# Plan times of all stages taken from a search, and the last projection issued in two parts

## The chip, the cores and the metric

The kernel runs on one core of a Trainium2 chip. The metric is the device time in microseconds of one execution. The kernel before takes 248.0 us, the median of three runs from 245.78 to 248.13. "Before" and "after" are the two kernels throughout. "Span" is the length of one traced execution; the timed run of the same execution is 1.7 us longer in all of them.

## The reference

Eight batches of windowed attention (8 heads, 576 positions, head size 64, window 32 to each side), then a gated feed-forward block with a convolution of three taps. All matmuls run in bf16 in the kernel.

```python
scores = scale * np.matmul(q, k.transpose(0, 1, 3, 2))
mask = np.abs(pos[:, None] - pos[None, :]) <= 32
attn = softmax(np.where(mask, scores, -1e9))             # shortened
x = np.matmul(attn, v)                                   # then [8, 576, 512]
h = np.maximum(x @ w_in, 0.0)                            # w_in 512 x 1024
conv_out = sum(conv_w[k] * h_shifted_by(k - 1) for k in range(3))   # shortened
out = (h * sigmoid(conv_out)) @ w_out                    # w_out 1024 x 512
```

## The kernel before

The kernel does not issue its instructions in program order. It first registers every piece of work as an `Op` with the engines that may do it, what it reads and writes, and a planned time `prio`. A list scheduler then walks a small model of the engines. At each step it finds the engine that could start something first, and among the operations that this engine could start within a slack, it takes the one with the lowest planned time. The result is one fixed order of instructions for each engine.

```python
TIMES = {
    "half": {(0, 0): (5.0, 9.0), (0, 1): (9.0, 9.0), (1, 0): (26.0, 7.0), (1, 1): (33.0, 7.0)},
    "piece": [(14.0, 1.0), (25.0, 0.6), (30.0, 0.8), (37.0, 0.8)],
    "chunk": 44.0, "step": 17.7, "margin": 7.0,
    "out": (25.0, 30.0, 31.0),
    "cast": {"w_in": 11.0, "w_out": 28.0},
    "load": ["qk00", "v00", "w_in0", "w_in1", "qk01", "v01", "qk10", "w_out0", "v10", "w_out1", "qk11", "v11"],
    "ahead": (9.0, 6.0), "cast_ahead": (0.5, 4.0),
}
# ... in Plan.place():
    lim = first[0] + self.SLACK[e]
    op = min((o for o in cand if opts[o][2] == e and opts[o][0] <= lim),
             key=lambda o: (o.prio, o.idx))
# ... in attention(b), for each half s:
    scores(b, s, 0, when(b, s, 0.32))
    scores(b, s, 1, when(b, s, 0.40))
# ...
    for g in range(NP):
        values(b, s, g, when(b, s, 0.58 + 0.1 * g))
```

The attention of a batch is done in two halves: casts on ACT or POOL, transposes of q and k on PE, scores (PE), exponentials (ACT), masks (DVE or POOL), values (PE), normalised copies `xn` (DVE), and a second transpose to `xT` (on PE for batches 0 and 1, as a DMA transpose from batch 2 on). Two batches make three chunks of 384 rows for the feed-forward part: hidden matmuls (PE), relu (ACT), convolution as matmuls with diagonal weights (PE), a third tap on DVE from chunk 2 on, tanh (ACT), a product (DVE), and the projection (PE, ACT copy, store). Chunks 0 and 1 are cut into two pieces each, numbered 0 to 3, so that work can begin early. `half` and `piece` place these stages, `out` places the three projections of chunk 0, `chunk` and `step` everything from chunk 2 on.

```python
def project(c, i, t):
    # ...
    def mm(e):
        for m in range(MB):                       # MB = 8
            nc.tensor.matmul(ps(sl, 0, d_model), gT[ig][:, m, 128 * i:128 * i + 128],
                             w_out_sb[:, m, :], start=(m == 0), stop=(m == MB - 1))
    add(pe(d_model, MB), t, mm,
        reads=[("gT", ig, m, (i, x)) for m in range(MB) for x in (False, True)]
        + [("w_out", m) for m in range(MB)], ...)
```

A projection is one operation of eight matmuls, so its first matmul waits for all eight blocks of `gT`. Where PE would idle in the first 36 us of the plan, `warm` puts "spin" matmuls whose result nobody reads.

The softmax here doesn't subtract the row's maximum and nothing guards it: scores larger than these inputs give would overflow.

## Time and profile before

All of the work on PE, priced at what single matmuls take in the trace, is 200.9 us. The table gives three marks in PE's stream. "Lost" is the time of the mark less the priced work that PE has done by then. The prediction shows how the prices come out of the profile.

| mark in the kernel before | time, us | work done, us | lost, us |
|---|---|---|---|
| first hidden matmul | 18.92 | 2.7 | 16.2 |
| piece 1 | 34.36 | 13.7 | 20.7 |
| chunk 2 | 73.70 | 43.9 | 29.8 |
| end of PE | 241.7 | 200.9 | 40.8 |
| end of span | 245.2 | | 44.3 |

Two thirds of the loss falls before chunk 2. What follows is 148 us of steady work with two engines near 70 to 77% and PE nearly full.

### The profile page before, as it was taken

The numbers are of one execution on the slowest core, as the hardware profiler recorded it, in microseconds if no ns is written. First come the engines' busy times: TensorE is split into PE (matmuls) and PEld (weight loads), VectorE is DVE, ScalarE is ACT, GpSimd is POOL, SyncE is SP. The second block draws the span as 40 slices with busy tenths as digits, with TensorE's granted clock in tenths as the row PEclk, the third lists the DMA queues.
The fourth block names the chain that finished last, engine by engine and source line by source line (L and its number), as shares of the span: only waits on it lengthen the run. The fifth ranks groups of instructions, "written<-read, shape, count | busy, mean of one in ns | idle before, by whom it ended". The sixth has DMA issues, their size and how long they took to land.

```text
span 245.2 us, 6624 instructions
## 1 busy us (share of the span) xinstructions
PE 223.2 (91%) x2532; PEld 136.3 (56%) x2562; DVE 175.3 (72%) x413; ACT 173.5 (71%) x351; POOL 155.4 (63%) x154
## 2 busy tenths in 40 slices
PE   4779789996989998999999999999899999999974
PEld 2438566775746564555465655555455555555531
DVE  7675773574888797859595958887886778667640
ACT  4678895799537888686868695878577786766641
POOL 3278789979998898999977749596836070000000
PEclk9999999999799999999999999999999999999999
DMA  5999999999987899969279975979623312321213
GB/s 179 253 401 244 271 307 266 281 311 277 253 183 194 225 237 258 254 174 261 67 247 182 233 188 178 194 220 184 168 41 100 88 43 67 78 86 43 88 43 128
DMA packets 68884, 45.93 MB, mean 187 GB/s; under 512 B 53980, under 2 KB 54004, under 8 KB 68852
## 3 DMA queue, kind: packets, MB, share of 16 engines
q1 hardware_dynamic: 68816, 45.50, 69.6%
q8 instruction: 20, 0.33, 0.6%
q14 instruction: 12, 0.10, 0.1%
q10 hardware_dynamic: 36, 0.01, 0.0%
HBM read 32.52 MB, written 9.44 MB: 171 GB/s over the span
## 4 chain that ended last, share of the span: by engine, by line
PE 76%; DVE 8%; ACT 5%; issue 3%; DMA 3%; POOL 2%; SPq 1%; ACTq 0%; POOLq 0%; DVEq 0%
PE ps_all L674 24%; PE ps_all L746 23%; PE ps_all L704 14%; PE ps_all L545 6%; PE ps_all L453 5%; PE ps_all L503 3%; DVE attn L527 3%; DMA vst<-in_v_dram 3%; ACT attn L516 2%; DVE gT L726 1%; ACT kT L263 1%; SPq L353 1%; POOL qn L265 1%; DVE xn L565 1%; PE ps_all L585 1%
## 5 line engine op out<-in xcount | busy, mean ns | idle before, releaser
L674 PE MATMUL ps_all<-xT,w_in_sb 128*128 128x385 bf16 (+4 forms) x448 | 77.1, 304 | 2.3 <-DVE xT L269 0.7
L746 PE MATMUL ps_all<-w_out_sb,gT 128*128 128x512 bf16 x262 | 65.0, 379 | 3.7 <-DVE gT L726 2.4
L726 DVE SCALAR_TENSOR_TENSOR gT<-ps_all,hT 128x384 bf16<-128x384 f32 (+3 forms) x112 | 54.1, 492 | 17.7 <-ACT ps_all L723 16.8
L527 POOL TENSOR_TENSOR attn<-attn,mask 128x1024 bf16<-128x1024 bf16 x24 | 51.3, 2158 | 20.4 <-ACT attn L516 15.8
L723 ACT ACTIVATE ps_all<-ps_all 128x384 f32<-128x384 f32 (+3 forms) x112 | 49.1, 445 | 20.1 <-DVE ps_all L719 14.2
L719 DVE SCALAR_TENSOR_TENSOR ps_all<-hT,conv_w_sb,ps_all 128x384 f32<-128x384 bf16 x80 | 48.4, 613 | 15.5 <-PE ps_all L704 14.6
L690 ACT ACTIVATE hT<-ps_all 128x385 bf16<-128x385 f32 (+4 forms) x112 | 48.9, 458 | 11.1 <-PE ps_all L674 8.6
L674 PEld LDWEIGHTS <-w_in_sb 128*128 128x128 bf16 x448 | 40.4, 98 | 22.5 <-issue 2.4
L704 PE MATMUL ps_all<-hT,diag_w 128*128 128x384 bf16 (+3 forms) x256 | 51.0, 300 | 0.3 <-ACT hT L690 0.2
L746 PEld LDWEIGHTS <-gT 128*128 128x128 bf16 x288 | 27.9, 97 | 32.7 <-issue 2.6
L265 POOL TENSOR_SCALAR vo<-vst 64x1024 bf16<-64x1024 f32 (+1 forms) x36 | 35.7, 993 | 10.4 <-DMA vst<-in_v_dram 7.7
L516 ACT ACTIVATE attn<-ps_all 128x1024 bf16<-128x1024 f32 (+1 forms) x40 | 37.1, 954 | 1.7 <-PE ps_all L503 1.2
L757 ACT COPY y<-ps_all 128x512 f32<-128x512 f32 x36 | 21.1, 588 | 22.2 <-PE ps_all L746 20.8
L565 DVE TENSOR_TENSOR xn<-ps_all,rec 128x256 bf16<-128x256 f32 (+1 forms) x64 | 29.4, 482 | 0.3
L265 POOL TENSOR_SCALAR ve<-vst 128x512 bf16<-128x512 f32 (+1 forms) x39 | 23.7, 619 | 3.9 <-DMA vst<-in_v_dram 3.4
L704 PEld LDWEIGHTS <-diag_w 128*128 128x128 bf16 x256 | 20.3, 98 | 9.1 <-issue 0.6
L263 ACT COPY kT<-ps_all 128x512 bf16<-128x512 bf16 (+1 forms) x30 | 21.9, 755 | 4.3 <-PE ps_all L453 4.3
L269 DVE COPY qT<-ps_all 128x512 bf16<-128x512 bf16 (+1 forms) x27 | 20.3, 763 | 2.7 <-PE ps_all L453 2.7
L527 DVE TENSOR_TENSOR attn<-attn,mask 128x1024 bf16<-128x1024 bf16 (+1 forms) x16 | 16.4, 1035 | 8.2 <-ACT attn L516 8.1
L545 PEld LDWEIGHTS <-attn 128*64 128x64 bf16 x640 | 14.1, 115 | 12.9 <-issue 7.1
L265 POOL TENSOR_SCALAR kn<-kst 128x1152 bf16<-128x1152 f32 (+1 forms) x18 | 17.9, 1000 | 5.2 <-DVE gT L726 2.6
L545 PE MATMUL ps_all<-ve,attn 128*64 128x65 bf16 x384 | 18.1, 202 | 2.6 <-DVE attn L527 1.1
(49 smaller groups left out, 170.5 us busy)
## 6 DMA issues: line engine op xcount, KB each, us to landing
qst<-in_q_dram SPq DMA_DIRECT2D x32, 288.0 KB, 5.3
kst<-in_k_dram SPq DMA_DIRECT2D x32, 288.0 KB, 5.1
out_dram<-y SPq DMA_DIRECT2D x36, 256.0 KB, 2.2
vst<-in_v_dram SPq DMA_DIRECT2D x23, 256.0 KB, 5.6
vst<-in_v_dram SPq DMA_DIRECT2D x16, 192.0 KB, 5.8
wst<-in_moe_w_in_dram SPq DMA_DIRECT2D x2, 1024.0 KB, 8.6
wst<-in_moe_w_out_dram SPq DMA_DIRECT2D x2, 1024.0 KB, 8.8
xT<-xn SPq DMA_TRANSPOSE x30, 3.1
```

What stands on the lines that cost most here:

```text
L265: nc.gpsimd.tensor_scalar(out=out_, in0=in_, scalar1=1.0, scalar2=0.0, op0=ALU.mult, op1=ALU.add)
L516: add(act(2 * w), t + 0.1, lambda e: nc.scalar.activation(at, ps(sl, 0, 1024).rearrange("p (e x) -> p e x", e=2)[:, :, 0:w], AF.Exp, bias= ...
L527: lambda e: ENG[e].tensor_tensor(out=x_, in0=x_, in1=m_, op=ALU.mult),
L545: nc.tensor.matmul(ps(sl, (D + 1) * (n * h_ + x), (D + 1) * (n * h_ + x + 1), 64 * j, 64 * j + 64), attn[a][:, 512 * h_ + col:512 * h_ + c ...
L565: add(dve(2 * n * D), t + 0.1, lambda e: nc.vector.tensor_tensor(out=xn[i][:, cs[0]:cs[0] + n].rearrange("p c (e g) d -> p c e g d", e=2)[ ...
L674: nc.tensor.matmul(ps(sl, 0, n), w_in_sb[:, kc, m * 128:(m + 1) * 128], x_[:, kc, a0:a1], start=(kc == 0), stop=(kc == KC - 1),)
L690: nc.scalar.activation(o_, i_, AF.Relu, bias=0.0, scale=0.5)
L704: nc.tensor.matmul(ps(sl, 0, no), diag_w[:, kk, m, :], hview(m, o0, o1, kk - 1), start=(kk == 0), stop=(kk == 2),)
L719: add(("DVE", no / 960.0 + 0.13), tt + 0.1, lambda e, m=m, mid=mid, pv=pv: nc.vector.scalar_tensor_tensor(out=pv(), in0=mid, scalar=conv_w ...
L723: add(act(no), tt + 0.2, lambda e, sl=sl: nc.scalar.activation(ps(sl, 0, no), ps(sl, 0, no), AF.Tanh, bias=0.0, scale=1.0), writes=[sl], s ...
L726: add(dve(no), tt + 0.3, lambda e, m=m, mid=mid, i2=i2, pv=pv: nc.vector.scalar_tensor_tensor(out=gT[ig][:, m, o0:o1].rearrange("p (i x) - ...
L746: nc.tensor.matmul(ps(sl, 0, d_model), gT[ig][:, m, 128 * i:128 * i + 128], w_out_sb[:, m, :], start=(m == 0), stop=(m == MB - 1),)
```

## The change

The intent is to let a search choose all planned times, instead of setting them by hand. It runs on the scheduler's own model with durations varied at random, so that the order found does not hang on exact durations. Constants that were fixed (phases within a half, lags within a chunk, slacks, early starts, the batches in which q and k copies are bound to an engine) become parameters. Besides, the projection of the last chunk is cut into matmuls 0 to 5 and 6 to 7, so that most of it need not wait for the last blocks of `gT`. No arithmetic changes.

```diff
-    "half": {(0, 0): (5.0, 9.0), (0, 1): (9.0, 9.0), (1, 0): (26.0, 7.0), (1, 1): (33.0, 7.0)},
-    "piece": [(14.0, 1.0), (25.0, 0.6), (30.0, 0.8), (37.0, 0.8)],
-    "chunk": 44.0, "step": 17.7, "margin": 7.0,
-    "out": (25.0, 30.0, 31.0),
-    "cast": {"w_in": 11.0, "w_out": 28.0},
-    "load": ["qk00","v00","w_in0","w_in1","qk01","v01","qk10","w_out0","v10","w_out1","qk11","v11"],
-    "ahead": (9.0, 6.0), "cast_ahead": (0.5, 4.0),
+    "half": {(0, 0): (27.75, 1.28), (0, 1): (-3.95, 3.99), (1, 0): (24.21, 2.64), (1, 1): (46.04, 3.6)},
+    "piece": [(-0.09, 1.6), (27.99, 0.33), (36.27, 0.86), (40.99, 2.81)],
+    "chunk": 56.82, "step": 15.6, "margin": 2.54,
+    "out": (15.31, 27.98, 29.58),
+    "cast": {"w_in": 11.95, "w_out": 32.67},
+    "load": ["qk00","v00","qk01","w_in1","v01","w_in0","qk10","w_out0","v10","w_out1","v11","qk11"],
+    "ahead": (5.65, 4.52), "cast_ahead": (11.32, 0.34),
+    "phase": (-0.13, 0.27, 0.32, 0.66, 0.67, -0.07, 1.2),   # was 0.05 .32 .40 .47 .58 .10 .98
+    "lag": (2.21, 2.77, 2.38),                              # was 1.4 2.7 2.6
+    "flex": (3, 2),                                         # was: bound for b > 1
+    "slack": (0.01, 0.03, 0.04, 0.49, 0.1),                 # was 0.05 0.1 0.1 0.3 0.3
+    "early": (0.0, 0.1, 0.0),                               # was 0.12 0.04 0.04
# ... in project():
-        def mm(e):
-            for m in range(MB):
+        for m0, m1 in ((0, 6), (6, MB)) if c == NCH - 1 else ((0, MB),):
+            def mm(e, m0=m0, m1=m1):
+                for m in range(m0, m1):
# ...
-        add(pe(d_model, MB), t, mm, reads=... all eight m ..., alloc=sl, group=gr)
+            add(pe(d_model, m1 - m0), t + m0, mm, reads=... m0 to m1 ...,
+                alloc=None if m0 else sl, group=gr if m1 == MB else None)
```

(Layout of the tables is drawn together; the rest of the diff passes the new parameters to the places where the constants stood.)

More of the change, by code (lines that the diff above doesn't have):

```diff
@@ L18 @@
 TIMES = {
-    "half": {(0, 0): (5.0, 9.0), (0, 1): (9.0, 9.0), (1, 0): (26.0, 7.0), (1, 1): (33.0, 7.0)},
-    "piece": [(14.0, 1.0), (25.0, 0.6), (30.0, 0.8), (37.0, 0.8)],
-    "chunk": 44.0,
-    "step": 17.7,
-    "margin": 7.0,
-    "out": (25.0, 30.0, 31.0),
-    "cast": {"w_in": 11.0, "w_out": 28.0},
-    "load": ["qk00", "v00", "w_in0", "w_in1", "qk01", "v01", "qk10", "w_out0", "v10", "w_out1", "qk11", "v11"],
-    "ahead": (9.0, 6.0),
-    "cast_ahead": (0.5, 4.0),
+    "half": {
+        (0, 0): (27.75, 1.28),
+        (0, 1): (-3.95, 3.99),
+        (1, 0): (24.21, 2.64),
+        (1, 1): (46.04, 3.6),
+    },
+    "piece": [(-0.09, 1.6), (27.99, 0.33), (36.27, 0.86), (40.99, 2.81)],
+    "chunk": 56.82,
+    "step": 15.6,
+    "margin": 2.54,
+    "out": (15.31, 27.98, 29.58),
+    "cast": {
+        "w_in": 11.95,
+        "w_out": 32.67,
+    },
+    "load": [
+        "qk00",
+        "v00",
+        "qk01",
+        "w_in1",
+        "v01",
+        "w_in0",
+        "qk10",
+        "w_out0",
+        "v10",
+        "w_out1",
+        "v11",
+        "qk11",
+    ],
+    "ahead": (5.65, 4.52),
+    "cast_ahead": (11.32, 0.34),
+    "phase": (-0.13, 0.27, 0.32, 0.66, 0.67, -0.07, 1.2),
[3 more added lines that the diff above has]
+    "early": (0.0, 0.1, 0.0),
 }
@@ L56 @@
     ENGINES = ("PE", "ACT", "DVE", "POOL", "SP", "ACTQ")
-    SLACK = {"PE": 0.05, "ACT": 0.1, "DVE": 0.1, "POOL": 0.3, "SP": 0.3, "ACTQ": 0.1}
     def __init__(self, banks=8):
@@ L90 @@
     LAT = {"PE": 0.22, "ACT": 0.16, "DVE": 0.13, "POOL": 0.2, "SP": 0.0, "ACTQ": 0.0}
-    EARLY = {"PE": 0.12, "ACT": 0.04, "DVE": 0.04, "POOL": 0.0, "SP": 0.0, "ACTQ": 0.0}
     def place(self):
@@ L105, in place @@
         free = {"PE": 1.5, "ACT": 2.8, "DVE": 3.9, "POOL": 3.3, "SP": 0.8, "ACTQ": 0.8}
+        early = dict(zip(("PE", "ACT", "DVE"), TIMES["early"]))
+        slack = dict(zip(self.ENGINES, TIMES["slack"] + (0.1,)))
         bank = [0.0] * (self.banks - 1) + [WARM[1]]
@@ L132, in place @@
                 for e, d in op.on.items():
-                    s = max(r + self.EARLY[e] if r > 0.0 else r, free[e])
+                    s = max(r + early.get(e, 0.0) if r > 0.0 else r, free[e])
                     if best is None or s + d < best[1] - 1e-9:
@@ L139, in place @@
             e = first[2]
-            lim = first[0] + self.SLACK[e]
+            lim = first[0] + slack[e]
             op = min(
@@ L443, in transposes @@
             sl = Slot(1)
-            t = when(b, s, 0.05 * n_)
+            t = when(b, s, TIMES["phase"][0] * n_)
             n = j1 - j0
@@ L466, in transposes @@
             on = dict([("ACT", 0.00095 * 128 * n + 0.1), ("DVE", 128 * n / 960.0 + 0.08)])
-            if b > 1:
+            if TIMES["flex"][0] <= b < TIMES["flex"][1]:
                 e = "ACT" if n_ % 2 else "DVE"
@@ L616, in attention @@
             transposes(b, s)
-            scores(b, s, 0, when(b, s, 0.32))
-            scores(b, s, 1, when(b, s, 0.40))
+            scores(b, s, 0, when(b, s, TIMES["phase"][1]))
+            scores(b, s, 1, when(b, s, TIMES["phase"][2]))
             if s == 1:
-                scores(b, s, None, when(b, s, 0.47))
+                scores(b, s, None, when(b, s, TIMES["phase"][3]))
             for g in range(NP):
-                values(b, s, g, when(b, s, 0.58 + 0.1 * g))
+                values(b, s, g, when(b, s, TIMES["phase"][4] + TIMES["phase"][5] * g))
             for c in ((0, 1), (2, 3, 4))[s]:
-                turn(b, c, when(b, s, 0.98 + 0.01 * c))
+                turn(b, c, when(b, s, TIMES["phase"][6] + 0.01 * c))
         if b == 0:
@@ L707, in mm @@
                     )
-            tt = t + (m + 1.4) * dt
+            tt = t + (m + TIMES["lag"][0]) * dt
             add(pe(no, len(TAPS(c))), tt, mm, reads=hk + [("diag", kk, m) for kk in TAPS(c)], writes=[sl], alloc=sl,
@@ L742, in project @@
         gr = []
-        def mm(e):
-            for m in range(MB):
-                nc.tensor.matmul(
-                    ps(sl, 0, d_model), gT[ig][:, m, 128 * i:128 * i + 128], w_out_sb[:, m, :],
-                    start=(m == 0), stop=(m == MB - 1),
-                )
-        add(pe(d_model, MB), t, mm,
-            reads=[("gT", ig, m, (i, x)) for m in range(MB) for x in (False, True)]
-            + [("w_out", m) for m in range(MB)],
-            writes=[sl], alloc=sl, slots=[sl], group=gr)
+        for m0, m1 in ((0, 6), (6, MB)) if c == NCH - 1 else ((0, MB),):
+            def mm(e, m0=m0, m1=m1):
+                for m in range(m0, m1):
+                    nc.tensor.matmul(
+                        ps(sl, 0, d_model), gT[ig][:, m, 128 * i:128 * i + 128], w_out_sb[:, m, :],
+                        start=(m == 0), stop=(m == MB - 1),
+                    )
+            add(pe(d_model, m1 - m0), t + m0, mm,
+                reads=[("gT", ig, m, (i, x)) for m in range(m0, m1) for x in (False, True)]
+                + [("w_out", m) for m in range(m0, m1)],
+                writes=[sl], alloc=None if m0 else sl, slots=[sl], group=gr if m1 == MB else None)
         r = NYY[0] % NY
@@ L798 @@
             if c == 0:
-                t = (25.0, 30.0, 31.0)[i]
+                t = TIMES["out"][i]
             else:
-                t = start[c + 1] + (2.7 + 2.6 * i) * dm
+                t = start[c + 1] + (TIMES["lag"][1] + TIMES["lag"][2] * i) * dm
             project(c, i, t)
```

## The prediction

> **What bounds the kernel now.** I read the page first (busy shares, the 40 slices, the groups), then busy time per stage in windows, then the chain of waits from 50 to 75 us, and last the timeline of the tail.
>
> ```profile
> span 245.2 us, 6624 instructions
> ...
> PE 223.2 (91%) x2532; PEld 136.3 (56%) x2562; DVE 175.3 (72%) x413; ACT 173.5 (71%) x351; POOL 155.4 (63%) x154
> ...
> PE   4779789996989998999999999999899999999974
> ```
>
> TensorE is the only engine that could be the bound as a whole, and after slice 12 it is nearly full. But 91% busy overstates it, as matmuls overlap. So I count columns. The page and the chain give unit prices: eight 512-wide output projections in 1.73 us (216 ns each), four 385-wide hidden matmuls in 0.66 us (165 ns), nine transposes in 0.50 us (56 ns), 32 score matmuls in 0.58 us (18 ns), 24 value matmuls in 0.50 us (21 ns). With these prices the whole useful stream (448 hidden, 256 convolution, 288 projection, 288 transposes, 576 scores, 640 values, 40 second transposes, without the spin matmuls that only keep the clock up) is 200.9 us. The span is 245.2, so 44.3 us are lost, and what the change can win is among these.
>
> ```profile
> 0.00:10.00 10.00, 5.09 (x24) 2.74 (x25) 7.29 (x43) 4.85 (x7) 2.46 (x9) 1.00 0.81 186
> 10.00:20.00 10.00, 7.85 (x100) 4.64 (x101) 6.08 (x13) 6.69 (x12) 7.14 (x11) 1.00 1.10 359
> 20.00:30.00 10.00, 8.47 (x138) 6.91 (x137) 7.37 (x15) 8.77 (x20) 8.47 (x13) 1.00 1.03 271
> 30.00:40.00 10.00, 8.92 (x161) 7.39 (x160) 7.33 (x20) 9.02 (x28) 8.13 (x12) 1.00 1.04 297
> 40.00:50.00 10.00, 9.78 (x118) 6.79 (x118) 4.48 (x14) 6.18 (x14) 9.51 (x13) 1.00 0.97 272
> 50.00:60.00 10.00, 8.15 (x155) 6.45 (x153) 5.26 (x10) 10.00 (x21) 8.60 (x8) 1.00 1.04 286
> ```
>
> Columns: PE, weight loads, DVE, ACT, POOL, clock, DMA share, GB/s. ACT is near full from 20 to 40 and wholly full from 50 to 60, with a hole of 3.8 us at 40 to 50. The hole is the plan's doing: there the 24 projections of chunk 0 run as one block (39.06 to 44.4), which feed ACT nothing but three copies. DMA is saturated to 60 us.
>
> Placing the useful work (by the order of matmuls in the program) against the trace: the first hidden matmul starts at 18.9 us with 2.7 us of work done, so 16.2 lost; piece 1 of chunk 0 at 34.4 with 13.7 done, 20.7 lost; piece 3 at about 51 with 29.3, 21.8 lost; chunk 2 at 73.7 with 43.9, 29.8 lost; the last chunk at 221.8 with 182.7, 39.1 lost. TensorE ends at 241.7 (40.8 lost), and 3.5 us of last copy and store follow. So 30 of 44 us go before chunk 2, 8 of them between 51 and 74. There the chain reads:
>
> ```profile
> 56.09 1.25 ACT kT L263 x2
> 57.34 0.90 ACT attn L516
> ...
> 58.26 0.97 DVE attn L527 x2
> ...
> 67.99 2.31 DVE attn L527
> ...
> 70.63 0.50 PE ps_all L585 x8
> ```
>
> Exponentials and masks of batch 1's second half come late; its last mask ends at 70.3, then come the transposes of xn, and only then can chunk 2 begin. From chunk 2 on the loss is 9.3 us in 148, thinly spread. In the tail TensorE waits for the last gT and then does all three projections:
>
> ```profile
> 234.04 0.82 PE L704 MATMUL ps_all<-hT,diag_w 128*128 128x384 bf16 x4
> 236.34 5.34 PE L746 MATMUL ps_all<-w_out_sb,gT 128*128 128x512 bf16 x23 [1.48 <-DVE gT L726]
> ```
>
> **The Trainium skill.** "TensorE: Matmul & The Clock Gate" (section "Wait — 56ns, not 53.3ns?") gives N over 2.4 GHz plus about 2.5 ns for a warm matmul, 215.7 ns at 512; the trace's 216 ns agrees, which is why columns may be priced. The same page ("The HAM clock gate") says an idle window of some 3.4 us drops the clock to half. The trace agrees loosely: the clock reads 0.71, 0.50 and 0.94 in the three 2-us windows from 60 us, after four microseconds in which PE was busy 60%, not idle; about 1.6 us are lost. "PSUM — Partial Sum Buffer" ("Engine vs sequencer instructions") says that ScalarE, VectorE and GpSimd queues are strict FIFO and matmuls complete in program order. So a badly placed instruction holds up everything behind it on its engine; the 24 projections ahead of other work at 39 us show it. "Perfetto Trace Analysis" ("Identifying the Most-Contended Engine") warns against matmul busy share as a measure; here 91% busy stands against 82% priced work.
>
> **The change, part by part.** No arithmetic goes. The instruction orders show the same 2,536 useful matmuls, 112 tanh, 112 relu, 40 masks; spin matmuls fall from 24 to 18. Spins only fill waiting time, so I count nothing for them.
>
> First, the head. Loads: the second half of batch 0's q and k now comes before w_in, and w_in's second half before its first. The transposes and scores of that half (1.7 us) are put before the first hidden matmul. Tracing it by the trace's durations: ACT casts two vo tiles (0.62 each) before the first exponential, so that starts near 12.6 instead of 11.98; two exponentials and two masks of 0.97 end near 15.5; the values of g=3,2 come first and need the second mask; then 9 transposes of k, copies (0.75), 40 scores, and the xn copies with a 1 us mask in between. First hidden near 21.3 instead of 18.9. Work done before it is 4.4, so 16.9 lost: 0.7 worse.
>
> Second, from there to piece 1: 8.7 us of TensorE work; ACT has 8 relu and 8 tanh of 0.36, 4 casts of w_in of 0.61, 3 copies of 0.73 and one of 0.58, some 11 us. ACT is the limit: piece 1 at 30 to 31, with 13.1 done, 17.4 lost against 20.7. The loss shrinks by 3.3 in total, though two exponentials (2 us of ACT) are now still to come.
>
> Third, piece 1 to chunk 2: 28 us of TensorE work and, summed from ACT's new order, 29.5 us of ACT (24 relu and 21 tanh of 0.2 to 0.3, 9 exponentials, 7 copies, 3 xT, 4 y). Before, the like took 39.3 us. The projection block now stands after all scores of batch 1, where ACT has its exponentials to do; piece 2's work follows piece 1 with no projections between. POOL's 35 us of casts and masks to the same point and the loads (about 11.3 MB up to w_out, which the trace had moved by about 41 us) allow it. At some 85% efficiency it takes 34 us: chunk 2 at about 65 instead of 73.7, with 41.0 done instead of 43.9. Lost 24.0 against 29.8: 5.8 us won, all head parts included.
>
> Fourth, the steady part: the same mix per chunk (9.3 us lost in 148). The order frees the choice of engine for q and k copies; ACT gets 9 copies more and DVE 8 fewer, some 6.5 us of work moved, neither engine at its limit there (both 70 to 77% busy). I give it 0.5 us.
>
> Fifth, the tail. The built order is 6, 6, 2, 6, 2, 2: twelve matmuls that need only m up to 5, 2.6 us, cover the 1.9 us that the last two convolutions need through DVE, ACT and DVE. So the wait of 1.48 us goes. Against it the last copies of 0.59 come 0.43 us apart and two stores overlap, some 0.4 us. Net 1.1.
>
> Sum: 5.8 + 0.5 + 1.1 = 7.4 us; span 245.2 to 237.8. The timed median is 2.8 us above the traced span, so 240.6 us.
>
> **The rivals.** (a) The head stays bound by its loads and by ACT: DMA share is 1.0 up to 60 us and ACT 10.00 of 10. Then the order cannot pull chunk 2 ahead by more than what the hole of 3.8 us gives; with the later first hidden the gain is 2 to 3 us, and the time 245. For it: exactly these two rows. Against: the hole itself, and the late chain at 51 to 74, which is order and not load. (b) In-order stalls: the plan was found on a model, and where real durations differ (a mask took 2.31 us at 67.99 against a mean of 1.04) every engine waits behind one misplaced item, such as 40 scores before the first hidden, or the projection block waiting for w_out. This would add 3 to 6 us in the head, and the time is 246 to 249. Jittered durations in the search speak against it. (c) The steady loss falls as well, from 9.3 to 5, and the clock drop at 60 us goes: 234 to 236. For it: a search over all stages should see the whole; against: the steady part has little idle left (0.2 to 0.7 us in 20).
>
> **Range and chances.** (a) and (b) have about one chance in four together, (c) one in six. So 240.6, range 235 to 246; faster by over 2% (below 243.0) 0.74, within 2% 0.24, slower 0.02.
>
> **What would show it.** Right: first hidden later (21 to 22 us), chunk 2's first 385-wide hidden at 62 to 67 us, no row of 10 us between 30 and 60 in which ACT falls to 6, no wait of PE for the last gT over 0.3 us, last copies 0.5 to 0.6 us apart. Wrong: chunk 2 at 70 or later, PE waiting over 2 us for w_out casts or kT copies in the head, or a loss beyond 11 us between chunk 2 and the end. The largest assumption is the 85% in the third step.

## The result, and the profile after

The kernel after takes 237.45 us (median of four runs, 237.19 to 238.5) against 248.06 for before in the same rounds. The ratio is 0.960, with a 95% interval of 0.953 to 0.966, and the result is correct. Ratios are the mean time of one kernel's fast runs over that of the other's of the same rounds, so they are not quite the ratio of the medians quoted. The traced spans are 245.2 and 235.7 us: 9.5 us less.

The head of the page after, and then the row of granted clock of the page before, which the prediction left out:

```profile
span 235.7 us, 6684 instructions
...
PE 222.7 (94%) x2556; PEld 134.6 (57%) x2556; DVE 169.1 (72%) x405; ACT 179.3 (76%) x360; POOL 154.8 (66%) x153
...
PE   3897999899989999999999999999999999999993
...
PEclk9999999999999999999999999999999999999999
```

```profile
PEclk9999999999799999999999999999999999999999
```

PE's busy time is the same (222.7 against 223.2) in a span 9.5 us shorter: idle time went, not work. The row of slices has its gaps filled in the first third. And the clock of before has a dent in slice 11 that after does not have; whether the plan has a part in that one stays open, and I come back to it.

The stages of the head in the kernel after (the columns are PE, weight loads, DVE, ACT, POOL, clock, DMA share, GB/s, as in the prediction's rows of before):

```profile
10.00:20.00 10.00, 8.75 (x142) 5.28 (x141) 5.84 (x14) 8.71 (x13) 6.24 (x10) 1.00 1.14 299
20.00:30.00 10.00, 9.37 (x126) 7.35 (x126) 7.70 (x19) 8.77 (x22) 8.46 (x14) 1.00 1.08 315
30.00:40.00 10.00, 9.94 (x174) 8.83 (x172) 6.83 (x22) 9.99 (x35) 6.97 (x10) 1.00 0.96 269
40.00:50.00 10.00, 9.17 (x129) 6.88 (x128) 7.77 (x18) 8.68 (x21) 9.75 (x13) 1.00 1.11 309
50.00:60.00 10.00, 9.82 (x157) 7.03 (x156) 6.13 (x16) 7.26 (x14) 9.67 (x10) 1.00 0.89 273
```

ACT's hole of 40 to 50 us is gone (8.68 instead of 6.18), and so is the stretch of 50 to 60 in which it was full; its work is spread, and PE is at 9.2 to 9.9 of ten from 20 us on. Chunk 2 can be told by its 385-wide hidden matmuls. The timeline of PE, before and then after:

```profile
73.70 0.83 PE L674 MATMUL ps_all<-xT,w_in_sb 128*128 128x385 bf16 x4
```

```profile
21.24 1.47 PE L699 MATMUL ps_all<-xT,w_in_sb 128*128 128x256 bf16 x12 [0.48 <-DVE xT L294]
...
30.86 1.97 PE L699 MATMUL ps_all<-xT,w_in_sb 128*128 128x129 bf16 x28
...
47.35 5.34 PE L771 MATMUL ps_all<-w_out_sb,gT 128*128 128x512 bf16 x24
...
62.60 1.48 PE L699 MATMUL ps_all<-xT,w_in_sb 128*128 128x385 bf16 x8
```

| mark | before: time, lost | after: time, work done, lost | predicted for after |
|---|---|---|---|
| first hidden | 18.92, 16.2 | 21.24, 4.4, 16.8 | 21.3, lost 16.9 |
| piece 1 | 34.36, 20.7 | 30.86, 13.1, 17.75 | 30 to 31, lost 17.4 |
| chunk 2 | 73.70, 29.8 | 62.60, 41.05, 21.55 | about 65, lost 24.0 |
| end of PE | 241.7, 40.8 | 232.02, 200.9, 31.1 | |

The first line says why the time of a mark alone misleads: the first hidden matmul comes 2.3 us later, but nearly as much work has been done before it. The third line of the timeline shows that the block of 24 projections is not gone: it has moved from 39.06 to 47.35 us.

What bounds the head now can be read from the chain of waits up to chunk 2 in the kernel after:

```profile
41.13 7.54 DMA vst<-in_v_dram
...
49.24 1.31 POOL kn L290
50.55 1.17 POOL ve L290 x2
...
54.76 1.16 POOL qn L290
...
55.97 0.40 PE ps_all L478 x4
```

The chain comes from a load of v (and before that from the load and the casts of w_out), through POOL's casts, to the transposes of q, and from there stays with PE. In the kernel before the chain at this place ran through exponentials and masks.

The tail after, PE and then ACT in one view each, followed by the first of before's last three copies, which stood 1.73 us apart:

```profile
226.02 0.82 PE L729 MATMUL ps_all<-hT,diag_w 128*128 128x384 bf16 x4
226.68 5.34 PE L771 MATMUL ps_all<-w_out_sb,gT 128*128 128x512 bf16 x24
```

```profile
229.90 0.59 ACT L782 COPY y<-ps_all 128x512 f32<-128x512 f32 x1 [1.69 <-PE ps_all L771]
231.63 1.07 ACT L782 COPY y<-ps_all 128x512 f32<-128x512 f32 x2 [1.14 <-PE ps_all L771]
```

```profile
238.26 0.59 ACT L757 COPY y<-ps_all 128x512 f32<-128x512 f32 x1 [2.04 <-PE ps_all L746]
```

The 24 projections start before the last convolutions are off the pipeline, with no wait. In before there were 1.48 us of it. The last two copies stand close together (1.07 us for two), so the end after PE is 3.7 us instead of 3.5. From the start of the last convolutions to the end of the span it is 11.16 us before and 9.68 after, a gain of 1.5 us net.

So the 9.5 us are: 8.2 before chunk 2, 1.5 in the tail, and -0.2 in the 150 us between. These are two single traces. Other traces of the same two orders lost 28.0 and 28.2 us by chunk 2 (e1 and e7, order of before) and 22.2 (e5, order of after; 24.7 in e2's slow execution of it), so the 8.2 is known to some 2 us only. Up to about 1.6 of it may belong to the dent of the clock; the experiments bear on that.

### The profile page after: what moved, and what is told of

Same layout as the page of the kernel before. It is cut to its first block, busy times and chain, and to the rows that moved or that the text cites. A ratio compares the mean times of both kernels' runs of the same rounds, so it can differ in the third digit from the quotient of the medians.

```text
span 235.7 us, 6684 instructions
## 1 busy us (share of the span) xinstructions
PE 222.7 (94%) x2556; PEld 134.6 (57%) x2556; DVE 169.1 (72%) x405; ACT 179.3 (76%) x360; POOL 154.8 (66%) x153
## 4 chain that ended last, share of the span: by engine, by line
PE 65%; DMA 13%; SPq 6%; POOL 5%; DVE 3%; issue 3%; ACT 2%; ACTq 0%; POOLq 0%
PE ps_all L771 21%; PE ps_all L699 21%; PE ps_all L729 11%; DMA vst<-in_v_dram 7%; PE ps_all L570 5%; PE ps_all L478 4%; DMA wst<-in_moe_w_out_dram 4%; PE ps_all L528 3%; SPq L378 3%; DMA kst<-in_k_dram 2%; SPq L409 2%; SPq L601 1%; POOL vo L290 1%; POOL ve L290 1%; POOL w_out_sb L290 1%
## 5 line engine op out<-in xcount | busy, mean ns | idle before, releaser
L699 PE MATMUL ps_all<-xT,w_in_sb 128*128 128x385 bf16 (+4 forms) x448 | 78.6, 304 | 1.2 <-ACT xT L288 0.7
L771 PE MATMUL ps_all<-w_out_sb,gT 128*128 128x512 bf16 x288 | 67.4, 379 | 0.0
L715 ACT ACTIVATE hT<-ps_all 128x385 bf16<-128x385 f32 (+4 forms) x112 | 49.7, 459 | 10.1 <-PE ps_all L699 9.5
L771 PEld LDWEIGHTS <-gT 128*128 128x128 bf16 x288 | 27.3, 98 | 29.5
L290 POOL TENSOR_SCALAR vo<-vst 64x1024 bf16<-64x1024 f32 (+1 forms) x34 | 33.0, 971 | 4.0 <-DMA vst<-in_v_dram 1.4
L290 POOL TENSOR_SCALAR kn<-kst 128x1152 bf16<-128x1152 f32 (+1 forms) x19 | 19.2, 1012 | 11.9 <-DMA kst<-in_k_dram 8.5
L729 PEld LDWEIGHTS <-diag_w 128*128 128x128 bf16 x256 | 21.2, 97 | 9.8 <-issue 0.3
L552 DVE TENSOR_TENSOR attn<-attn,mask 128x1024 bf16<-128x1024 bf16 (+1 forms) x16 | 15.0, 944 | 8.9 <-ACT attn L541 8.8
L570 PEld LDWEIGHTS <-attn 128*64 128x64 bf16 x640 | 13.3, 111 | 11.6 <-issue 9.2
L290 POOL TENSOR_SCALAR qn<-qst 128x1152 bf16<-128x1152 f32 (+1 forms) x18 | 18.7, 1045 | 0.7 <-PE ps_all L699 0.2
L570 PE MATMUL ps_all<-ve,attn 128*64 128x65 bf16 x384 | 17.4, 197 | 0.8 <-ACT hT L715 0.7
L288 ACT COPY qT<-ps_all 128x640 bf16<-128x640 bf16 (+1 forms) x24 | 17.4, 754 | 0.3
```

The lines of the kernel that those rows point to most:

```text
L290: nc.gpsimd.tensor_scalar(out=out_, in0=in_, scalar1=1.0, scalar2=0.0, op0=ALU.mult, op1=ALU.add)
L552: lambda e: ENG[e].tensor_tensor(out=x_, in0=x_, in1=m_, op=ALU.mult),
L570: nc.tensor.matmul(ps(sl, (D + 1) * (n * h_ + x), (D + 1) * (n * h_ + x + 1), 64 * j, 64 * j + 64), attn[a][:, 512 * h_ + col:512 * h_ + c ...
L699: nc.tensor.matmul(ps(sl, 0, n), w_in_sb[:, kc, m * 128:(m + 1) * 128], x_[:, kc, a0:a1], start=(kc == 0), stop=(kc == KC - 1),)
L715: nc.scalar.activation(o_, i_, AF.Relu, bias=0.0, scale=0.5)
L729: nc.tensor.matmul(ps(sl, 0, no), diag_w[:, kk, m, :], hview(m, o0, o1, kk - 1), start=(kk == 0), stop=(kk == 2),)
```

## The experiments

All were correct, and all ran three to five rounds beside the kernel before. Variants are written in the changed source with old values put back. With all old values and no split, the order built is that of the kernel before on every engine. Each expectation names its own theories. The three groups of parameters used below are: **loads** (`load`, `cast`, `ahead`, `cast_ahead`), **head** (`half`, `piece`, `out`), **steady** (`chunk`, `step`, `margin`, `lag`, `phase`).

| run | median (range, runs), us | ratio to before, 95% interval | span, us | chunk 2: time, lost |
|---|---|---|---|---|
| e1 split alone | 245.39 (243.68 to 248.45, 6) | 0.9995 [0.990, 1.009] | 242.0 | 71.94, 28.0 |
| e2 after, no split | 239.64 (237.97 to 241.65, 6) | 0.9745 [0.968, 0.981] | 239.9 | 65.76, 24.7 |
| e3 loads on before | 243.68 (241.96 to 243.92, 4) | 0.991 [0.984, 0.998] | 242.1 | 70.51, 26.3 |
| e4 late block on before | 242.59 (240.35 to 243.51, 4) | 0.987 [0.979, 0.995] | 240.9 | 64.18, 25.0 |
| e5 after again | 238.34 (235.77 to 239.66, 6) | 0.963 [0.956, 0.970] | 236.2 | 63.23, 22.2 |
| e6 after, old loads | 243.51 (243.07 to 244.34, 4) | 0.988 [0.982, 0.994] | 241.9 | 73.70, 27.3 |
| e7 before, spins doubled | 247.14 (244.80 to 248.30, 6) | 1.001 [0.995, 1.008] | 243.5 | 72.13, 28.2 |
| e8 after, no spins | 239.90 (238.94 to 240.29, 4) | 0.974 [0.967, 0.981] | 237.2 | 63.92, 22.9 |
| e9 after, old steady | 243.35 (243.03 to 244.25, 4) | 0.984 [0.978, 0.990] | 241.3 | 70.50, 27.3 |
| e10 after, old head | 242.67 (241.84 to 244.51, 4) | 0.982 [0.975, 0.989] | 240.2 | 58.24, 20.5 |
| e11 after, block spread | 237.36 (236.63 to 237.88, 6) | 0.959 [0.954, 0.964] | 235.9 | 62.57, 22.4 |
| e12 loads and steady on before | 240.46 (240.00 to 241.34, 4) | 0.972 [0.965, 0.979] | 239.0 | 60.38, 22.7 |

The kernel before had 11 runs beside each of three sets (e1 to e4, e5 to e8, e9 to e12), each set on one chip: medians 247.56, 247.44 and 248.02.

### The split by itself: e1 and e2

e1 adds only the split to the kernel before; e2 takes only the split from the kernel after.

```diff
-        for m0, m1 in ((0, MB),):                                          # before
+        for m0, m1 in ((0, 6), (6, MB)) if c == NCH - 1 else ((0, MB),):   # e1; e2 is the reverse
```

> The kernel before, with nothing changed but the last projection in two parts (the built order is the same up to the last 24 matmuls). My theory: the wait of TensorE for the last gT (1.48 us before) goes, and 0.3 to 0.5 us of it is given back because the last two copies come 0.43 us apart and two stores overlap: 0.8 to 1.3 us faster. The rival: the end is set by the last copies and stores, which then run into each other, so that less than 0.4 us is won.

> The kernel after with the last projection in one part again, plan times kept (same order up to the last 24 matmuls). My theory: 0.8 to 1.3 us slower than the kernel after (so a ratio to the kernel before of about 0.964 instead of 0.960), all of it in a wait of TensorE for the last gT. The rival: as in the other run, under 0.4 us.

The timing of e1 says nothing either way (ratio 0.9995 with an interval of nearly 2%). The trace does, for e1's order is that of before up to the last 24 matmuls. The ends of PE's timeline, e1 and then e2:

```profile
232.26 0.82 PE L706 MATMUL ps_all<-hT,diag_w 128*128 128x384 bf16 x4
232.91 5.34 PE L748 MATMUL ps_all<-w_out_sb,gT 128*128 128x512 bf16 x24
```

```profile
228.81 0.82 PE L706 MATMUL ps_all<-hT,diag_w 128*128 128x384 bf16 x4
231.12 5.34 PE L748 MATMUL ps_all<-w_out_sb,gT 128*128 128x512 bf16 x24 [1.48 <-DVE gT L728]
```

With the split the projections follow the convolutions at once, without it comes the wait of 1.48 us, in either plan. From the last convolutions to the end it is 9.74 us (e1) and 9.68 (after) with the split, 11.16 (before) and 11.09 (e2) without. The split is worth 1.4 us in the traces, a little over the 0.8 to 1.3 expected, in either plan. The timed runs agree, though they are not all of one chip: e2's four fast runs at a mean clock of 0.999 or more have a mean of 239.1 us, those of after (seven, counting e5 below, at 0.998 or more) 237.5. The trace of e2 must not be compared as a whole. It is of an execution with a dent in the clock at 22 to 28 us, and lost 24.7 by chunk 2 instead of 21.55 with the same order.

### One group on the kernel before: e3 and e4

```diff
-    "cast": {"w_in": 11.0, "w_out": 28.0},                                 # e3
-    "load": ["qk00","v00","w_in0","w_in1","qk01","v01","qk10","w_out0","v10","w_out1","qk11","v11"],
-    "ahead": (9.0, 6.0), "cast_ahead": (0.5, 4.0),
+    "cast": {"w_in": 11.95, "w_out": 32.67},
+    "load": ["qk00","v00","qk01","w_in1","v01","w_in0","qk10","w_out0","v10","w_out1","v11","qk11"],
+    "ahead": (5.65, 4.52), "cast_ahead": (11.32, 0.34),
```

> The kernel before with only four of the new plan values: the order of loads, the two cast times, and the two lead times of loads and casts. All stage times stay old. In the built order the first hidden matmul then has 4.4 us of work before it (as in the kernel after) and the 24 projections of chunk 0 move from behind 18.3 to behind 28.2 us of work, so the block moves with no stage time changed. My theory as predicted (stage times make the gain, the loads only allow it): at most 3 us faster, since the phases, steps and half times are the old ones. The rival, that the loads are what moves the head: 5 us or more faster, and chunk 2 begins at 66 us or earlier with 44.2 us of work done.

The new loads alone win 0.9%, of some 4%. They lost 26.3 us by chunk 2, 3.5 less than before did and 1.7 less than e1, which has before's order up to there. (Each of these traces has dents ahead of chunk 2: one in e3, at 17.5 to 20.9 us, one in before, two in e1.) PE then waits for POOL's casts of q (1.9 us at the longest): new loads under the old planned times do not meet the work that they are for.

```diff
-    "out": (25.0, 30.0, 31.0),
+    "out": (50.0, 50.5, 51.0),                                             # e4
```

> The kernel before with only the three plan times of chunk 0's projections raised from 25 to 31 up to 50 to 51, loads unchanged. In the built order the block begins behind 22.2 us of work instead of 18.3 and batch 1's second-half scores come earlier (behind 28.8 instead of 32.0). My theory, that the hole of 3.8 us in ACT behind an early block and the late scores cost the 8 us between 51 and 74 us: 3 to 5 us faster, ACT without a row under 8 in 40 to 50. The rival, that the loads and their casts hold the head: within 1.5 us of the kernel before.

The same row as that with before's hole of 6.18, in e4:

```profile
40.00:50.00 10.00, 10.00 (x153) 7.75 (x151) 6.63 (x20) 7.67 (x20) 9.50 (x13) 1.00 1.10 289
```

Only half of the hole is filled (7.67; I had expected at least 8), PE is full, and 1.3% is won (3.6 us by the means of fast runs, inside the 3 to 5 expected). This shows that the block of projections at 39 us did cost time in the kernel before. It does not show by which way: when it moves, the scores of batch 1 come earlier too (from 32.0 to 28.8 us of priced work ahead of them), and the two are not separated.

### The clock and the loads: e5 to e8

e5 is the kernel after again, as a control on this chip.

> The kernel after once more, unchanged, as the control on this chip: ratio 0.955 to 0.967. By the theory that the kernel before loses part of its time to clock drops, which vary from run to run (its eleven last runs range from 244.5 us at mean clock 1.000 to 249.9 at 0.978), the runs of this kernel lie within 1.5 us of each other at a clock of 0.997 or more. The rival, that the drops are chance and fall on both kernels: a spread of 4 us or more here too.

It repeats the result: 0.963, with 22.2 us lost by chunk 2. The expectation on its spread failed: its six runs range over 3.9 us, from 235.77 (clock 0.998) to 239.66 (0.992), and one of 239.35 had 0.999. So this kernel meets a drop of the clock too, if rarely, and most of its spread comes without one.

e6 is the kernel after with the old group of loads (e3's diff, reversed).

> The kernel after with the old order of loads, cast times and lead times of loads and casts; all else new. In the built order the first hidden matmul stands behind 2.7 us of work again, the 24 projections of chunk 0 behind 17.7 us, the second-half scores of batch 1 behind 33.6. If the gain of the head is mainly the order that the loads decide (block and scores), most of it goes: 242 us or more. If the loads are worth what they gave alone on the kernel before (0.9%), it is 2 to 3 us slower than the kernel after, 239.5 to 240.5.

Windows and timeline of e6:

```profile
40.00:50.00 10.00, 9.46 (x107) 6.21 (x105) 3.87 (x13) 4.96 (x13) 9.67 (x13) 1.00 1.00 290
```

```profile
73.70 0.83 PE L676 MATMUL ps_all<-xT,w_in_sb 128*128 128x385 bf16 x4
```

The hole in ACT is back (4.96), and chunk 2 starts at 73.70, to the digit where before has it, though with 2.5 us more work done by then. All of e6's timed runs had the full clock, so the clock has no part in it. Without the new loads the new plan keeps little of its gain: the mean of e6's runs is 243.6 us, against 237.5 for the fast runs of the kernel after. As e3 won only 0.9% with them, loads and plan must be set together.

e7 asks whether the dent of the clock is a matter of PE being idle, by doubling the spins of before; e8 takes all spins from after.

```diff
-            for _ in range(n):
+            for _ in range(2 * n):        # e7;   e8: range(0)
```

> The kernel before with two spin matmuls for each one (48 instead of 24, all in the first 36 us). If the clock drops of the head come from too little TensorE activity there, the mean clock rises to 0.993 or more in every run and the median falls by 1 to 2 us, to about 246. The rival: the added spins stand in front of real work in TensorE's queue, and the time stays or grows by 1 to 3 us.

> The kernel after without any spin matmul, all else in the same order. If activity holds the clock, the mean clock falls to 0.97 to 0.985 and the time rises by 2 to 5 us over the kernel after. The rival, that the denser new order holds the clock by itself, as my prediction took for granted when it counted nothing for the spins: within 1 us of the kernel after.

The dent in the trace of before, in windows of 2 us:

```profile
58.00:60.00 2.00, 1.24 (x24) 1.09 (x24) 1.74 (x2) 2.00 (x6) 1.92 (x3) 1.00 0.98 281
60.00:62.00 2.00, 1.35 (x42) 1.27 (x42) 1.86 (x9) 1.00 (x5) 1.92 (x2) 0.71 0.91 293
62.00:64.00 2.00, 2.00 (x44) 1.57 (x44) 0.90 (x3) 1.11 (x3) 1.92 (x4) 0.50 0.97 338
64.00:66.00 2.00, 1.74 (x29) 1.53 (x25) 1.96 (x9) 1.35 (x4) 1.84 (x3) 0.94 1.26 235
```

e7's timing did not move (1.001), and its six runs had mean clocks of 1.0, 1.0, 0.993, 0.984, 0.993 and 0.986: the dents did not go. The spins fill only the first 36 us of the plan, and the dent of before's trace lies at 60. But the execution of e7 that was traced happened to have none. In it chunk 2 stands at 72.13 with 28.2 lost, 1.6 less than the 29.8 of before, which is what the prediction read off the windows as the cost of the dent. A third trace warns against taking this as settled: e1 has the same order up to there and two dents (10.9 to 14.3 and 58.7 to 62.1 us), and lost only 28.0. What a dent costs depends on where it falls, and one trace of an order differs from the next by as much.

Of e8's expectations, the slowdown came true and its reason did not. The reported clock stays at 0.998 or more without spins, yet the kernel is slower than e5, by 1.0 us in the traces, by 2.4 us in the means of fast runs on the same chip (239.8 against 237.4) and so by 1.1% in the ratios. The first hidden matmuls of e8 and of e5:

```profile
21.75 2.72 PE L676 MATMUL ps_all<-xT,w_in_sb 128*128 128x256 bf16 x12 [0.78 <-DVE xT L271]
```

```profile
21.13 1.47 PE L699 MATMUL ps_all<-xT,w_in_sb 128*128 128x256 bf16 x12 [0.78 <-DVE xT L294]
```

The same twelve matmuls take 2.72 us instead of 1.47. Without spins PE runs at about half its rate until about 24 us, while the clock column of these windows reads 1.00. In e5 the nine transposes at 5.53 us take 1.14 us and the nine at 8.94 us 0.68, so there the change to full rate came by 9 us. With spins, too, the moment differs between executions: in the trace of after, the nine transposes at 9.26 us still take 1.14 us and five spins at 12.21 us take 2.31, and the nine at 14.32 us, with 0.97, stand at the change. By chunk 2 the traces of e8 and e5 are only 0.7 us apart in loss.

How much of the whole gain do the dents make? The kernel before ran 33 times in these sets, 23 fast. Among the fast runs, six had a mean clock of at least 0.998, with a mean of 244.8 us; six near 0.993 had 246.4, and eleven near 0.985 had 247.3. The mean of all 23 is 246.4. The kernel after ran ten times, eight of them fast, all of these at 0.997 or more, with a mean of 237.5. The steps have a reason that the clock records of the traces show: all ten dents ahead of PE's end in the traces of these runs are alike, 3.41 to 3.42 us at half clock (in before's trace from 60.85 to 64.26 us). One costs 1.7 of some 245 us of clock, so a mean of 0.993 is one dent, 0.985 two and 0.978 three; the six runs of before at 0.977 to 0.979, all of them slow, have a mean of 249.2 us. That is some 1.5 us for each dent on average, with much scatter: the fast runs near 0.993 range from 244.74 to 247.79, those near 0.985 from 245.25 to 248.25.

Without dents the kernels are 244.8 - 237.5 = 7.3 us apart. The other 246.4 - 244.8 = 1.6 us go with before having dents and after hardly any. This is observed and not tried: no kernel of mine took the dents away from before, so why the plan after meets fewer of them stays open. PE is busy only 1.20 and 1.24 of 2 us ahead of the dent in before's trace, which would suit an idle PE as the cause. But the traces speak against so simple a rule. In e7 PE is less busy still at this place, 2.20 of 4 us, and no dent follows:

```profile
57.00:61.00 4.00, 2.20 (x36) 1.78 (x32) 2.11 (x3) 4.00 (x9) 3.83 (x4) 1.00 0.90 226
```

In e5, the kernel after itself, PE is busy 1.66 of 4 us from 12 to 16 us, and the clock stays (the nine transposes at 16.01 us take 0.68 us). What the runs do show is that the plan matters: e6 and e8 have no dent in four runs each, by their clocks, while e9 and e10 below have one or two in every run (e11, on the chip of these two, in one run of six).

### Which times matter: e9 to e12

e9 and e10 take one group from the kernel after: e9 puts back the old `chunk`, `step`, `margin`, `lag` and `phase`, e10 the old `half`, `piece` and `out`.

```diff
-    "chunk": 56.82, "step": 15.6, "margin": 2.54, ...                      # e9
+    "chunk": 44.0, "step": 17.7, "margin": 7.0, ...
```

> The kernel after with the old chunk start, step, margin, lags and phases (the values that place the steady part and the order within each half attention). Theory one, from the priced work (9.3 us lost between chunk 2 and the end of TensorE before, 9.5 after, 1.4 of the former in the tail): these values win nothing after chunk 2, so the loss from chunk 2 to TensorE's end stays within 1 us of 9.5, and the whole is at most 3 us slower than the kernel after (238 us), by the phases in the head. Theory two: the search has tuned the steady part as well; the loss after chunk 2 grows by 2 us or more, and the whole is 4 us or more slower.

```diff
-    "half": {(0, 0): (27.75, 1.28), (0, 1): (-3.95, 3.99), ...}, "piece": ..., "out": ...   # e10
+    "half": {(0, 0): (5.0, 9.0), (0, 1): (9.0, 9.0), ...}, "piece": ..., "out": ...
```

> The kernel after with the old times of the four first half attentions, of the four pieces and of chunk 0's projections; loads, steady values and planner slacks new. In the built order chunk 2 begins behind 37.7 us of work instead of 41.0 and the block behind 28.4. Theory one: loads alone on the kernel before left 26.3 us lost at chunk 2 against 21.6 in the kernel after, and these stage times make that difference; then 25 us or more are lost at chunk 2 here, and the whole is 3 to 5 us slower than the kernel after. Theory two: loads and phases suffice; then 23 us or less are lost at chunk 2 and the time is within 1.5 us of the kernel after.

(The 9.3 us that this expectation gives for before run only to the last chunk; to PE's end before loses 11.0.) The mean of e9's runs is 243.5 us, 6.0 more than after's. A good part of it comes with dents: the clocks of its runs are 0.984 to 0.991, one or two dents each, so some 2 us as an estimate from the 1.5 us above. All that the trace shows of it is lost before chunk 2, where 27.3 are lost instead of 21.55, and both dents of this trace lie there (18.4 to 21.8 and 62.8 to 66.2 us), for an estimated 3 of these 5.75 us. From chunk 2 to PE's end it loses 9.4 us, as the kernel after does (9.5). So theory one was right about the place and too low about the size, and the "steady" parameters win nothing in the steady part. They can act through the head: the phases set the order of masks, values and copies within a half, there too, and chunk 2's planned time decides what in the head it competes with.

e10 shows the other side. It has the lowest loss of all at chunk 2 (20.5), and its mean of 242.9 us is still 5.4 more than after's, since 15.1 us are lost later, instead of 9.5. The chain of waits of e10 and its longest stage behind chunk 2:

```profile
75.90 1.26 SPq L578
...
77.21 5.30 DMA xT<-xn
82.51 2.27 PE ps_all L676 x8
```

```profile
70.00:85.00 15.00, 11.31 (x131) 6.31 (x132) 10.69 (x22) 8.24 (x16) 12.86 (x12) 0.93 1.01 197
```

Chunk 2 comes early, but batch 2's attention, which chunk 3 needs, is late. Its DMA transpose takes 5.30 us on the chain, and PE is busy 11.31 of 15. The 0.93 in this row is a dent, from 83.0 to 86.4 us, after 4 us in which PE was busy 1.20; all four runs of e10 had one, by their clocks of 0.990 to 0.993, so an estimated 1.5 of the 5.4 us go with it. My mechanism for e10 (a late chunk 2) was wrong, although the total came out about as expected. It also says that being early at chunk 2 is not the aim in itself; the measure holds only while the work behind it is ready.

e11 spreads chunk 0's projections in the kernel after, so that they no longer stand as a block.

```diff
-    "out": (15.31, 27.98, 29.58),
+    "out": (40.0, 48.0, 56.0),                                             # e11
```

> The kernel after with chunk 0's three projections planned at 40, 48 and 56 instead of 15 to 30, so that the block of 24 matmuls is cut in three by transposes, scores and values. My prediction held the hole that such a block leaves in ACT to be costly; in the kernel after the block is still there (ACT waits 1.14 us twice between 49 and 53 us). If the hole costs, this is 1 to 2 us faster than the kernel after, below 237 us, ratio 0.952 to 0.958. The rival: TensorE is full through the block and ACT is not the limit there any more, so within 0.7 us of the kernel after, or slower where the cut order brings a new wait.

Its row of 50 to 60 us:

```profile
50.00:60.00 10.00, 9.37 (x155) 6.17 (x155) 6.38 (x19) 6.94 (x15) 8.90 (x8) 1.00 0.78 223
```

ACT is no busier (6.94 against 7.26) and the time is the same, 237.36: the rival's outcome. The block costs nothing that shows any more in the kernel after. e11 is not distinguishable from the kernel after, so there is no better version here.

e12 puts loads, steady and split on the kernel before, with its old planned times of the head and its old slacks.

> The kernel before with the new loads, the new steady values and the split, but with the old half, piece and projection times and the old slacks of the planner. Beside the run with the loads alone (242 to 244 us) and the run of the kernel after less its head times it tells what the steady values and the slacks do. If loads and steady values (with the phases) carry the gain: 239 to 240.5 us, 23 us or less lost at chunk 2. If the head times are needed: 241 us or more, 25 us or more lost at chunk 2 (of which the split still takes 1.4 from the whole).

It gets 2.8% of the 4%: 22.7 lost by chunk 2, but 11.7 from there to PE's end, against 9.5 in after. As in e10, the early chunk 2 is paid for in part by what follows.

e12 and e10 differ only in the planner's own constants, `flex`, `slack` and `early`: old in e12, new in e10. With the old head times the new constants are 2.3 us slower (242.9 against 240.6 by the means, same chip and rounds, no run of one within the range of the other). No run puts the old constants into the kernel after, so what they do with the new head times is not known.

Taken from the kernel after one at a time, loads, steady and head cost 6.1 (e6), 6.0 (e9) and 5.4 us (e10) by the means of fast runs: 17.5 us together, where the whole change wins 246.4 - 237.5 = 8.9. Without the dents it would be some 14 against 7.3, as an estimate from the shares above. So the groups depend on each other, though loads alone do win something (e3), and the gain cannot be shared out among them.

## Why the prediction was right

It said 240.6 us, range 235 to 246, most likely faster by over 2%. It came to 237.45. The mechanism held in its main steps; several sizes were off, and one hit had a wrong reason.

- **First hidden at 21.3, 0.7 us more lost.** Right: 21.24, 0.6 more. e5 has it at 21.13, and e2, a slow execution of the same order, at 23.32.
- **Piece 1 at 30 to 31, 17.4 lost.** Right in number: 30.86 and 17.75. The reason given, that ACT is the limit there, is not borne out: from 21.24 to 30.86 us ACT is busy 8.39 us and PE 9.47 of 9.62.
- **Piece 1 to chunk 2 in 34 us "at some 85% efficiency".** This was the mis-sized term, and the one that the prediction called its largest assumption. Its sum slipped as well: 34 us for 28 us of work is 82%, and 85% would be 33. The trace has 31.7 us for 27.9 us of work, 88%. So chunk 2 lost 21.55 instead of 24.0, and the head gave 8.2 us instead of 5.8. The direction was right, and so was the place. As the 29.8 us of before hold its dent and the 24.0 allow for none, the dent's going was counted in the 5.8 without being said.
- **The reason given for it.** Half right. The 24 projections do follow the scores of batch 1 and the hole at 40 to 50 is gone; e4 shows that the block's old place cost something. But ACT falls to 7.26 in 50 to 60, just above my limit of 6, and in e11, where the block is cut up, ACT is no busier and the time is the same. What matters more than I had thought is the order of the loads, which I only checked for being possible: without it (e6) 27.3 us are lost by chunk 2, near the 28.0 to 29.8 of before's order.
- **Steady part, 0.5 us.** Wrong, though small: -0.2 in the traces. e9 agrees, with the same loss behind chunk 2 under the old values.
- **Tail, 1.1 us net.** Right in mechanism, and 1.4 to 1.5 in size: I charged 0.4 us for the crowded end, and it is 0.2.
- **From span to timed median, 2.8 us.** Wrong. It is 1.7 in every traced run; the other 1.1 was no more than the distance of before's traced execution (246.88 us) from the median, within a spread of over 4 us. The predicted span of 237.8 was 2.1 us too high, and this step added the other 1.1.

Of the rivals, (a), a head bound by its loads, is true of the kernel after as a description (its chain runs through a load of v and POOL's casts) but not in what it would have made of the time. Of (b), misplaced items, after's trace shows none of note; e3 and e10 show what they look like. (c) asked for a lower steady loss and for the dent to go. The first did not happen. The second did in the traced execution and in most others, and some 1.6 us of the mean gain go with it. I gave (c) one chance in six for both together and should have held them apart.

## What to carry to other kernels

Compare plans by lost time at a mark (time less the priced work done by then), not by when a mark is reached, and check the loss behind the mark too: e10 was the earliest and among the slower ones. Parameters of a list scheduler act together, so taking out one group shows that it is needed, not what it is worth. Where a gain of a few per cent is at stake, look at the clock of every run of both kernels: here nearly a fifth of the mean gain (1.6 of 8.9 us) goes with how often it dropped. And where runs of one order differ by 2 us at a mark, one trace of each kernel does not settle a cause of that size.

## What the Trainium skill lacked or had wrong

- "TensorE: Matmul & The Clock Gate", section "The HAM clock gate", names an idle window of about 3.4 us as what returns PE to half rate; its section "A second HAM failure mode: psum-queue depth-cycling" adds frequent short idle times, without saying how much. In the kernel before the clock fell to 0.50 after 4 us in which PE was busy 61% (1.20 and 1.24 of 2 us), and it did not fall after 55% in e7 (2.20 of 4 us) or 41% in e5 (1.66 of 4 us). So a PE that works more than half of the time can lose its clock, a quieter one can keep it, and no busy share alone decides; the page does not say what does.
- The same page warns that the profiler's clock events can be unreliable. It does not say that the cold state at the start can be missing from them: in e8 the clock reads 1.00 from 15 to 22 us, while twelve matmuls of 256 columns take 2.72 us and in e5 1.47. The duration of a known matmul is the safer sign. The page's two rates (1.2 and 2.4 GHz) do agree: as an estimate from them, 12 x 256 columns are 2.56 and 1.28 us, before latency.
- No page that I found has the spread that such drops in the middle of a kernel make from run to run on one core: 244.33 to 249.86 us in 33 runs of the kernel before, whose fast runs are slower on average the lower their mean clock (0.998 or more: 244.8; 0.993: 246.4; 0.985: 247.3), one step for each drop of 3.41 us.
